# A gated mix of a spectral filter and a state-space recurrence: the issue order of all engines replaced by another one

## The chip, the cores and the metric

The kernel runs on one core of one Trainium2 chip. The metric is the device time of one execution in microseconds; a kernel's time is the median of several executions. The engines are TensorE (PE; its weight loads are PEld), VectorE (DVE), ScalarE (ACT), GpSimd (POOL) and SyncE (SP), which here only issues DMA transfers. Each engine takes its instructions strictly in the order in which they were issued, and waits at the first one whose inputs or buffers are not there.

## The reference

The input x has 2048 rows (time) and 1024 columns (features), in bf16. Two branches are computed from it and mixed by a gate of each row:

```python
g = sigmoid((x * gate_w).sum(-1, keepdims=True))
# a: spectral filter
X = rfft2(x.astype(float32), axes=(-2, -1)) * (w_r + 1j * w_i)
a = irfft2(X, s=(S, D)).astype(bfloat16)
# b: diagonal complex recurrence over the 2048 rows
h_t = Lam_bar * h_{t-1} + B_bar @ x_t
b_t = 2 * real(C @ h_t) + x_t * Dskip
out = g * a + (1 - g) * b
```

Lam_bar = exp(exp(log_dt) * Lambda) and B_bar = (Lam_bar - 1) / Lambda * B. The recurrence has 1024 complex states.

## The kernel before

The spectral branch is a chain of matrix products. x is turned on TensorE (L936, L938, tiles pt) and copied to xQ by VectorE (L947), folded (L961 to L972), transformed along the features (fd, L442 to L455, with the cast X1 on ScalarE, L461), and transformed along the rows in two steps (s1, L474, with the cast of L489; then s2, L609, after a round trip through DRAM; cast X2, L619). It is multiplied by the filter on VectorE (times_w, UV, L632), and transformed back in two steps: is1 (L648, cast C1 at L656, stored at L662 to a scratch in DRAM, read again as raw at L670) and is2 (L681, cast ZT on ScalarE, L690). Last come the groups called id (L825, L829), which ScalarE scales by the gate into BT or raw (L836) and VectorE puts together (Z and R, L844 to L865).

The recurrence branch works in 8 units of rows. The input products psu (L410, 1024 matmuls) are cast to h (L420). Each unit then goes through a list of small steps on VectorE: multiplication by tables (L340, L343), joins (L346, L349), carries (L354, L359, L380), fold_in (L362), the scan itself (L368), fill_in (L376), and the two outputs out_re (L383) and out_im (L387). One step, called next (L372), is on ScalarE between the scan and fill_in: it copies the scan's ends into the places from which fill_in reads. A step in the kernel's text is one "piece" of the list PIECES.

The products with C give y. For the tiles of 128 rows 0 to 9 they are made early: ps_y (L732, L738), scaled by the gate's other half into ye (ScalarE, L763) and stored to y_scratch in DRAM (SP, L773). The skip term is xs (loaded at L782 on SP), multiplied on VectorE (L788), scaled on ScalarE into su (L798) and added to y_scratch by an accumulating DMA issued by POOL (L804). Later POOL adds y_scratch to the finished spectral tiles (L870), and SP stores the result (L878). There are two buffers of ye and two of su: a third ye waits until a store has been read out, a third su until an accumulating DMA has. The last tiles are made at the end (ps_q, L746) and added by VectorE (L911, L918) and stored (L924).

At the start, four tables for the recurrence are made by ScalarE's sine and exponential steps (L281, L1133, L1134, L1136, L295, L296), fed by VectorE (L1129, L1131).

The order in which all of this is issued is not left to a scheduler. Three tables at the top of the file set it. ORDER is a string of some 980 characters; each stands for one kind of work (the dict `acts`), and each occurrence takes the next step of that kind, so that the letters' order is the order of issue on all five engines at once. PIECES is the order in which the letter v takes the recurrence's pieces. SLOTS says for each PSUM tile in turn which of the four PSUM slots it gets. A slot is taken by the next tile only when the last one in it has been read, so SLOTS and ORDER belong together.

```python
    for act in "".join(ORDER):
        if act == "v":
            piece(next(pieces))
        else:
            next(acts[act], None)
```

The engines wait on each other by semaphores, which are set from the data and the buffers; ORDER does not change what is computed.

Of the kernel before, what the change touches and what calls it, by code (L numbers as in the profile page):

```python
# [41 lines left out]
TURN_DVE = tuple(range(16))  # L42
CLOSES = (0, 1, 2, 3, 10, 4, 5, 11, 12, 6, 7, 8, 9)
PIECES = (
# [7 lines left out]
)  # L52
SLOTS = (
    "0123012301230123021302130231023102302302130230123013021302301201320320213023021310102312012301230210",
    "2302021302130230230213132012031203203123120310321032103210130212031203120",
)
MIRROR = (6, 7, 8, 9)
ORDER = (
    "xTxUfTUVfVVa|2xTTGfVVVrrffa|tfUUtGGFFaxEfftffTTxUESbSbtfU2fFTaxAxTffUUfrFAE2fftxSaakFtEAEtfxbbbbbtTT",
    "TFtTbEbUUbFSUUf~ttfFEufSUUU1UbSSArESttfFAAAftFtbbbttEEwttthH~tfthfftufFFSHbtAtttvfvEEtvgvbSASKhtt1r1",  # L60
    "AtAe1vttrtHtr~1vftve111~htuuhttvtFrttF1ttvtHfvthh1vv1tttEttvcEvccccvccctHvSevvSSFcHHwFAAhhEwScKvE11v",
    "KvvSccctttvvtvvAhKvHeevhvcccvv1nAA1KK1swHvvvvvHHsYvvvvkMvvvvssssvhvvvvvHvvnnLYYsvvvvvvnNWssJNsJNNvsh",
    "MhsvsvvJvsvWyHMss344jhvvMM3hHvLvv5vWmm++HnH54v56nMyvvMMWv78378v4nnmmJNvJNvv5hv5vJ56Yvhv4NJyNjYvM+vvM",
    "453WM787HH44y55hH+mm67h8Hv+n7vWm3Nn54JWYvvnvv558468+vvvhMv3vmvJj5NMMv77+8484vYnJN+ydmvyN55JWvvvHhd6h",
    "3H787mM8Hvv555+mjn6M44hYN77vv+5vm3n55HJv644dvyJ8n87N7+Jmv5v5v5vvv+8vh6NnYvym7vv878Hh8qhq+mNviqJivHh+",
    "miiiIqIniv+vHHvIIvvYyivvIJXv+IvvqvYvvnIqviXNvyiJnimqiIinmvYNIiihIIIvvvvvvvJvvNNvq%iiIIIIv++hHHlzlvpp",
    "hvllzZZPZZZZPRRQQRRRmXvHdJhRpzzDmD+ZZRZZHvPZZlJQvoRpOvQvPlDzBzZZovZvOlZpovRYRZlZDzzvvoRRBDoOOvoyQRQB",
    "BlvDDv+POBZOZRBZZvZvlZzzpvZZQDoovvQoDCZYZZooZ9PooYRyRRRDyYRRQQ9CC9000999DDD09000",
)

EVEN = ((0, 0), (2, 1), (2, 0), (0, 1))
# [1167 lines left out]
```

## Time and profile before

| | us |
|---|---|
| median of 3 executions | 301.17 |
| lowest and highest of them | 300.79, 302.21 |
| the profiled execution's own time | 303.33 |
| its span in the profile | 301.6 |
| TensorE busy | 292.6 (97%) |
| VectorE busy | 284.2 (94%) |
| ScalarE busy | 209.5 (69%) |
| GpSimd busy | 81.0 (27%) |
| granted TensorE clock | 1.000 |

The profile's page gives the busy time of every engine, groups of instructions by line, and the chain of work that ended last. A row of a timeline has the start, the duration, the engine, the line and the operation with its tiles (out<-in), and in square brackets the idle time ahead of it and what ended that. A row of the list of waits has the engine, the tile and line that waited, what it waited for, and the total, the number and the longest of such waits. A row of the table by windows has the stretch and its length, then for each engine its busy time and instructions in it, then the granted clock, the share of the DMA engines and GB/s. A DMA row's duration in the chain is from issue to landing.

### The profile page before, as it was taken

How to read it: one execution, taken by the hardware profiler on the slowest of the kernel's cores; microseconds unless marked ns; L12 is line 12 of the kernel's file. 1: busy time of each engine (PE TensorE's matmuls, PEld its weight loads, DVE VectorE, ACT ScalarE, POOL GpSimd, SP SyncE). 2: the span in 40 equal slices, each digit the busy share in tenths (PEclk: the TensorE clock that was granted, in tenths of full speed). 3: DMA queues.
4: the chain of work that ended last, by engine and by line, in shares of the span. 5: the costliest groups of instructions: out<-in, count | busy, mean ns of one | idle time of the engine just before them, and what ended most of it. 6: DMA issues, size and time to landing. Idle time of an engine off the chain costs nothing. (4 is left out here: it accounts for less than half of the span.)

```text
span 301.6 us, 6230 instructions
## 1 busy us (share of the span) xinstructions
PE 292.6 (97%) x2446; PEld 194.6 (65%) x2446; DVE 284.2 (94%) x359; ACT 209.5 (69%) x323; POOL 81.0 (27%) x107
## 2 busy tenths in 40 slices
PE   7899999999999999999999999999979999999995
PEld 4465868977764874477546754688547996556443
DVE  4999999999889999999988999999997899999994
ACT  1899999998531578757685989757969885267100
POOL 2232276696460020200310111201111042244230
PEclk9999999999999999999999999999999999999999
DMA  6999999999978779878995895878999419999995
GB/s 216 289 281 202 196 159 311 153 142 175 196 213 242 196 181 237 211 217 208 222 275 161 180 256 124 195 229 251 250 225 189 79 19 193 124 184 193 124 163 190
DMA packets 74140, 59.21 MB, mean 196 GB/s; under 512 B 44872, under 2 KB 61664, under 8 KB 74112
## 3 DMA queue, kind: packets, MB, share of 16 engines
q1 hardware_dynamic: 66560, 49.69, 64.8%
q0 software_dynamic: 6896, 8.69, 23.8%
q8 instruction: 19, 0.31, 0.5%
q10 hardware_dynamic: 656, 0.44, 0.5%
q14 instruction: 9, 0.07, 0.1%
HBM read 27.33 MB, written 23.08 MB: 167 GB/s over the span
## 5 line engine op out<-in xcount | busy, mean ns | idle before, releaser
L410 PE MATMUL psu<-xQ,BT 128*128 128x256 bf16 x1024 | 116.2, 273 | 0.0
L410 PEld LDWEIGHTS <-BT 128*128 128x128 bf16 x1024 | 98.9, 98 | 16.9 <-issue 4.2
L732 PE MATMUL ps_y<-CT,h 128*128 128x512 bf16 x416 | 93.6, 380 | 0.7 <-ACT ye L763 0.6
L732 PEld LDWEIGHTS <-h 128*128 128x128 bf16 x416 | 39.8, 98 | 47.9 <-issue 4.0
L804 POOL DMA_DIRECT2D y_scratch<-su x20 | 19.2, 987 | 122.9 <-ACT su L798 84.8
L420 ACT CAST h<-psu 128x1024 bf16<-128x1024 f32 x32 | 32.3, 1013 | 15.3 <-PE psu L410 14.6
L343 DVE TENSOR_TENSOR h<-h,tab 128x4096 bf16<-128x4096 bf16 (+1 forms) x20 | 37.4, 1870 | 0.2
L368 DVE TENSOR_TENSOR_SCAN h<-rz,h 128x512 bf16<-128x512 f32 (+1 forms) x14 | 35.9, 2584 | 0.1
L340 DVE TENSOR_TENSOR xQ<-h,tab 128x4096 bf16<-128x4096 bf16 x12 | 27.4, 2284 | 0.3 <-ACT h L420 0.2
L763 ACT ACTIVATE ye<-ps_y,omg 128x512 f32<-128x512 f32 x26 | 17.2, 682 | 12.3 <-PE ps_y L732 6.1
L372 ACT ACTIVATE xQ<-h,r_sb 128x254 bf16<-128x254 bf16 x48 | 20.5, 508 | 1.4 <-DVE h L368 1.4
L870 POOL DMA_DIRECT2D BT<-y_scratch x10 | 12.7, 1543 | 32.1 <-ACT h L420 16.7
L746 PE MATMUL ps_q<-CT,h 128*128 128x512 bf16 (+2 forms) x112 | 20.9, 349 | 0.0
L836 ACT ACTIVATE BT<-ps_id,gB 128x1024 bf16<-128x1024 f32 x14 | 14.9, 1114 | 6.0 <-DMA out_dram<-BT 6.0
L656 ACT CAST C<-ps_is 128x1024 bf16<-128x1024 f32 x16 | 15.6, 1011 | 4.6 <-PE ps_is L648 3.8
L798 ACT ACTIVATE su<-xs,omg 128x512 f32<-128x512 bf16 x20 | 14.1, 722 | 6.7 <-DVE xs L788 3.0
L619 ACT CAST X<-ps_s 128x1024 bf16<-128x1024 f32 x16 | 16.1, 1008 | 3.8 <-PE ps_s L609 2.6
L690 ACT CAST ZT<-ps_is 128x1024 bf16<-128x1024 f32 x16 | 16.8, 1125 | 0.6 <-ACT su L798 0.6
L746 PEld LDWEIGHTS <-h 128*128 128x128 bf16 x112 | 10.4, 98 | 10.5
L461 ACT CAST X<-ps_fd 128x1024 bf16<-128x1024 f32 x16 | 15.8, 1019 | 0.4 <-PE ps_fd L455 0.4
L289 POOL CAST tab<-sc 128x512 bf16<-128x512 f32 x4 | 4.9, 1234 | 23.3 <-ACT sc L1136 23.3
L947 DVE COPY xQ<-pt 128x1024 bf16<-128x1024 bf16 x12 | 7.8, 683 | 3.5 <-PE pt L938 3.5
(210 smaller groups left out, 440.8 us busy)
## 6 DMA issues: line engine op xcount, KB each, us to landing
y_scratch<-ye SPq DMA_DIRECT2D x20, 256.0 KB, 3.9
y_scratch<-su POOLq DMA_DIRECT2D x20, 256.0 KB, 6.5
Bb<-turn_scratch SPq DMA_DIRECT2D x16, 256.0 KB, 4.9
turn_scratch<-C SPq DMA_DIRECT2D x16, 256.0 KB, 3.4
raw<-turn_scratch SPq DMA_DIRECT2D x8, 512.0 KB, 5.0
xs<-in_A_x_dram SPq DMA_DIRECT2D x13, 256.0 KB, 4.4
out_dram<-BT SPq DMA_DIRECT2D x11, 256.0 KB, 4.5
CT<-in_A_x_dram SPq DMA_DIRECT2D x5, 512.0 KB, 4.7
```

Of the source, the lines that this page charges most:

```text
L340: nc.vector.tensor_mul(out=tmps["s"], in0=u[:, :, ::-1], in1=bc(i))
L343: nc.vector.tensor_mul(out=u, in0=u, in1=bc(i))
L368: nc.vector.tensor_tensor_scan(out=seg, data0=flat(rz, i), data1=seg, initial=0.0, op0=ALU.mult, op1=ALU.add)
L372: nc.scalar.activation(out=tmps["s"][:, 0, :, i, 1:TS], in_=u[:, 1, :, i, 0:TS - 1], func=ACT.Copy, scale=r2_sb[:, js.start + i:js.start + ...
L410: nc.tensor.matmul(psu[:, j, :], lhsT=BT[4 * q + j][:, ri, d8, :], rhs=xQ[:, c, d8, :], start=(d8 == 0), stop=(d8 == 7))
L420: nc.scalar.copy(out=hs[c][:, :, ri, 4 * q:4 * q + 4].rearrange("p e b (q j) -> p e b q j", j=16), in_=psus.pop((c, q, ri)).rearrange("p b ...
L619: nc.scalar.copy(out=X2s[g][:, :, b], in_=ps2s[g][b])
L690: nc.scalar.copy(out=fft["ZT"][:, kp, :, :, 2 * G:2 * G + 2], in_=pszs.pop((G, kp)).rearrange("p v (x n) -> p x n v", n=64))
L732: nc.tensor.matmul(psy, lhsT=hs[c][:, tq, ri, jb, :], rhs=CT[ri][:, jb, 512 * dh:512 * (dh + 1)], start=(i == 0), stop=(i == 15 and tb not ...
L746: nc.tensor.matmul(psq, lhsT=hs[c][:, tq, ri, jb, :], rhs=CT[ri][:, jb, at:at + n], start=(i == 0), stop=(i == 15))
L763: nc.scalar.activation(out=ye, in_=psys[tb][:, K * hf:K * (hf + 1)], func=ACT.Copy, scale=omg[:, tb:tb + 1])
L804: nc.gpsimd.dma_start(out=y_dram[tb, hf], in_=xgs[tb, hf], accum_op=ALU.add)
```

## The change

The three tables are replaced as a whole; no other line differs. The change comes with the words "Order of all engines laid anew from the last trace's durations, judged by four cases with longer transfers". The first line of each, before and after:

```diff
 PIECES = (
-    0, 1, 2, 3, 4, 5, 6, 9, 8, 10, 7, 11, 12, 13, 14, 15, 16, 18, 17, 20, 21, 22, 23, 19, 24, 25, 26, 27, 28, 29, 30,
...
+    0, 1, 2, 3, 5, 6, 8, 4, 7, 9, 10, 11, 12, 14, 13, 15, 16, 18, 17, 20, 21, 19, 24, 23, 25, 22, 26, 27, 29, 28, 30,
...
 SLOTS = (
-    "0123012301230123021302130231023102302302130230123013021302301201320320213023021310102312012301230210",
...
+    "0123012301230132013012031023103210321021302130210312013213023020132102030231231021032312032101321301",
...
 ORDER = (
-    "xTxUfTUVfVVa|2xTTGfVVVrrffa|tfUUtGGFFaxEfftffTTxUESbSbtfU2fFTaxAxTffUUfrFAE2fftxSaakFtEAEtfxbbbbbtTT",
...
+    "xxTUffTUV2VVxGf|Va|VVGTffattfUtTfataGFUfaxxr2kbFraxxxfrETTUxSESfttfAUAFET2fFtff1tTTUfFTFETUUffbbbUEt",
```

What the tables do is seen in the rows of an engine's program. A row has the line, the operation, its output and inputs, and the output's shape; the number behind a tile's name is a running one and differs between the two programs for the same tile.

On ScalarE, in the first 15 us, before: the sine step for small vectors, then the two casts X1 of fd's first tiles (L461), then three steps of the first table.

```order
L1134 ACTIVATE SC_158<-ang2_153 128x16
L461 CAST X1_285<-ps_fd_264 128x1024
L461 CAST X1_318<-ps_fd_273 128x1024
L1133 ACTIVATE rot_kk_292<-ang_255 128x512
L1134 ACTIVATE sc_291<-ang_255 128x512
L1136 ACTIVATE SC_158<-a2_kk_250,chpi_117 128x16
L489 CAST CT0_82<-ps_s1_320 128x1024
```

After, in the same place:

```order
L1134 ACTIVATE SC_158<-ang2_153 128x16
L1133 ACTIVATE rot_kk_250<-ang_243 128x512
L1134 ACTIVATE sc_249<-ang_243 128x512
L1136 ACTIVATE SC_158<-a2_kk_240,chpi_117 128x16
L461 CAST X1_317<-ps_fd_271 128x1024
L461 CAST X1_344<-ps_fd_291 128x1024
L1136 ACTIVATE sc_249<-rot_kk_250,chpi_117 128x512
L489 CAST CT0_82<-ps_s1_339 128x1024
```

The three table steps (L1133, L1134, L1136) have moved from behind the two casts to in front of them.

On SP, near 205 us of the trace before. The rows with ye are the stores of tile 7 (its two halves), those of L670 are the loads raw that is2 reads, those of L782 the loads of xs:

```order
L670 DMA raw_125<-turn2_scratch_58 128x2048 x3
L773 DMA y_scratch_60<-ye_2798 128x512
L670 DMA raw_125<-turn2_scratch_58 128x2048
L782 DMA xs_3034<-in_A_x_dram 128x1024
L773 DMA y_scratch_60<-ye_2902 128x512
L1182 DMA_TRANSPOSE xQ_121<-in_A_x_dram 128x8x128
L670 DMA raw_125<-turn2_scratch_58 128x2048
```

After:

```order
L670 DMA raw_125<-turn2_scratch_58 128x2048 x2
L773 DMA y_scratch_60<-ye_2797 128x512
L670 DMA raw_125<-turn2_scratch_58 128x2048
L782 DMA xs_3036<-in_A_x_dram 128x1024
L773 DMA y_scratch_60<-ye_2938 128x512
L670 DMA raw_125<-turn2_scratch_58 128x2048 x4
```

The store of the first half has moved one raw load forward (it stood behind three and stands behind two), the store of the second half too: before it stood behind the fourth raw load and an xs load, and now it stands behind the third and an xs load. The further raw loads follow it.

On VectorE, at the end of the last unit of the recurrence, from its fill_in (L376) on, before:

```order
L376 TENSOR_TENSOR h_3312<-h_3312,xQ_121 128x2048
L863 TENSOR_TENSOR BT_122<-BT_122 128x2x512
L340 TENSOR_TENSOR xQ_121<-h_3312,tab_123 128x4096
L865 TENSOR_TENSOR BT_122<-BT_122 128x2x512
L343 TENSOR_TENSOR h_3312<-h_3312,tab_123 128x4096
L844 TENSOR_TENSOR BT_122<-BT_122 128x2x2x128
L846 TENSOR_TENSOR BT_122<-BT_122 128x2x2x128
L387 TENSOR_TENSOR h_3312<-h_3312,xQ_121 128x2x1024
L383 TENSOR_TENSOR h_3312<-h_3312,xQ_121 128x2x1024
L911 SCALAR_TENSOR_TENSOR xQ_121<-xs_3174,omg_142,BT_122 128x1024
L855 TENSOR_TENSOR BT_122<-BT_122 128x4x256
L857 TENSOR_TENSOR BT_122<-BT_122 128x4x256
```

After:

```order
L376 TENSOR_TENSOR h_3259<-h_3259,xQ_121 128x2048
L340 TENSOR_TENSOR xQ_121<-h_3259,tab_123 128x4096
L343 TENSOR_TENSOR h_3259<-h_3259,tab_123 128x4096
L911 SCALAR_TENSOR_TENSOR xQ_121<-xs_3254,omg_142,BT_122 128x1024
L383 TENSOR_TENSOR h_3259<-h_3259,xQ_121 128x2x1024
L844 TENSOR_TENSOR BT_122<-BT_122 128x2x2x128
L387 TENSOR_TENSOR h_3259<-h_3259,xQ_121 128x2x1024
L846 TENSOR_TENSOR BT_122<-BT_122 128x2x2x128
L855 TENSOR_TENSOR BT_122<-BT_122 128x4x256
L857 TENSOR_TENSOR BT_122<-BT_122 128x4x256
L918 SCALAR_TENSOR_TENSOR raw_125<-ps_q_3743,omg_142,xQ_121 128x512
```

The sum L911 has moved from behind out_im and out_re (L387, L383) to in front of both, with the other steps of Z and R laid differently around them, and out_re goes before out_im.

More of the change, by code (lines that the diff above doesn't have):

```diff
@@ L44 @@
 PIECES = (
[7 rows of a table removed]
[7 rows of a table added]
 )
 SLOTS = (
-    "0123012301230123021302130231023102302302130230123013021302301201320320213023021310102312012301230210",
-    "2302021302130230230213132012031203203123120310321032103210130212031203120",
+    "0123012301230132013012031023103210321021302130210312013213023020132102030231231021032312032101321301",
+    "3202132032103203203120201230123023021321302130213021031203103212031202310",
 )
@@ L58 @@
 ORDER = (
-    "xTxUfTUVfVVa|2xTTGfVVVrrffa|tfUUtGGFFaxEfftffTTxUESbSbtfU2fFTaxAxTffUUfrFAE2fftxSaakFtEAEtfxbbbbbtTT",
[L60 to L68, printed above, removed]
+    "xxTUffTUV2VVxGf|Va|VVGTffattfUtTfataGFUfaxxr2kbFraxxxfrETTUxSESfttfAUAFET2fFtff1tTTUfFTFETUUffbbbUEt",
+    "SSEffAAFfUrt~fFTuUUUUffEbrbUttttbtbSbbttESASSbfAAbbbbAFEFEhttSAtffttt~uHhH~bftFEtFttutgttKSSv1th1EFe",
+    "11tv1111fv~tvA1rwAttvhhtht1cefEtvtvrcStttcStvvttvvccreHcHutttvtfvvHtvA1tHhttvFcccAvwwccFEEhhvvvSvttS",
+    "vvccFtvvvhvHvccHvAvvvvecKK1vv1vKA1KvEwSAKv1evsYYHHhHvvvvshnHvvMLvsssnvvvnnNWJvvWvsssvMhvvNvvjvsJvsvM",
+    "sshvhNyHHvsvsvkNssvWv3MvLhYMMvvnm4v4JmY5yJ++3HMHmvvn544NNJWJ5vv678v5v+vnvMm3v54vMnM56hh74+NvN8v3vyj5",
+    "78mvH+5vhh5678mvvnMvHWH445Jdd77vMYHNYWy+vJ34nm4jmN8+MJ556vnvy7+8Yvv53W4v7585nNhhJvNMvH4vm8+vJvWvv677",
+    "Hhvvv5jHmM3Mn5+454XJ86ymvN787Yhm8385vJ55H4n4Nvy6n+57hv8v5567vvvmvvvYyNnv7hvvvJ8878HhvX++mq+hqHvNmmiH",
+    "HvIJiIiIvnvvviqivivYvJynvIqvvIIviINi+vvvvqq+nmvmiqiiNniIYyIIIvJhJvNiivqivNvIYvvvHvIIiIIdv%XhvHlzlzJp",
+    "Pvl+ZZZpPm+ZZZRRzhQlzHdJvpPRhRpollQDDmHRZZ+RPZZRZvZQQDOovyvDlzzvRBvoZYZOBvpzlzoZZovDRZ+RZQQRRvOZoOlZ",
+    "vvRZZvBBRlDDooDZZQvvPvvOCBOBvzzZpQvoPZZDoZ9ZZQQY0RRRRyyRRC999CDDoo0o9099DY00D00Y",
 )
```

12 rows, old and new, of the table PIECES are left out of this document.

## Prediction

> **What bounds the kernel now.** I read the page's shares first, then the table by windows, then the timelines of the engines around each hole that the table shows, and last the chain of waits where the largest hole lies.
>
> ```profile
> span 301.6 us, 6230 instructions
> PE 292.6 (97%) x2446; PEld 194.6 (65%) x2446; DVE 284.2 (94%) x359; ACT 209.5 (69%) x323; POOL 81.0 (27%) x107
> ```
>
> TensorE is busy for 292.6 of 301.6 us, VectorE for 284.2. Both columns are nearly full, so the order can't win more than the holes that TensorE has. The table by windows shows where they are: each row is a stretch, and TensorE's hole is its length less its busy time.
>
> ```profile
> 0.00:10.00 10.00, 7.20 (x58) 4.51 (x59) 5.55 (x21) 2.95 (x9) 3.44 (x16) 1.00 0.76 240
> 10.00:20.00 10.00, 9.61 (x80) 5.51 (x79) 9.93 (x24) 9.96 (x15) 1.72 (x1) 1.00 1.11 305
> 120.00:150.00 30.00, 29.57 (x266) 18.38 (x265) 29.82 (x24) 21.14 (x33) 3.69 (x5) 1.00 0.88 209
> 150.00:200.00 50.00, 49.70 (x425) 29.56 (x425) 47.65 (x39) 39.54 (x69) 6.71 (x8) 1.00 0.79 197
> 220.00:240.00 20.00, 18.32 (x174) 14.04 (x173) 18.48 (x12) 16.71 (x25) 1.73 (x2) 1.00 0.86 177
> 280.00:302.00 22.00, 18.39 (x102) 9.09 (x99) 17.63 (x26) 0.01 (x1) 3.34 (x3) 1.00 0.80 158
> sum 302.00, PE 292.61 PEld 194.58 DVE 284.19 ACT 209.54 POOL 81.01; mean PE 24.38 PEld 16.21 DVE 23.68 ACT 17.46 POOL 6.75
> ```
>
> The table was cut so that it covers 302 us, and the holes are 302.00 − 292.61 = 9.4 us. Of these 2.80 lie in the first 10 us, where the first loads arrive, and 3.61 in the last 22, nearly all behind the last matmul, where the last tile is scaled and stored. Neither can be laid anew away. That leaves 0.39 + 0.43 + 0.30 + 1.68 = 2.8 us in between, and 1.68 of it in one place, 220 to 240 us. The granted clock (third column from the end) is 1.00 throughout. The Trainium skill, page "Perfetto Trace Analysis", section "Identifying the Most-Contended Engine", holds that busy share says little of how far TensorE is from its limit, because matmuls are pipelined, and would have us judge by the share of weight loads: 65% here, which by that rule would leave a third of the span open. The trace does not bear that out for an order alone: a change of order removes no matmul and no weight load, only holes.
>
> **The change part by part.** The code is the same; only the order is laid anew, and with it which PSUM slot a tile gets. Four places decide.
>
> The first is the start. ScalarE, VectorE and TensorE there, before:
>
> ```profile
> 11.72 1.91 ACT L461 CAST X<-ps_fd 128x1024 bf16<-128x1024 f32 x2
> 13.51 0.64 ACT L1133 ACTIVATE rot_kk<-ang 128x512 f32<-128x512 f32 x1
> 14.04 0.63 ACT L1134 ACTIVATE sc<-ang 128x512 f32<-128x512 f32 x1
> 14.56 0.30 ACT L1136 ACTIVATE SC<-a_kk,chpi 128x16 f32<-128x16 f32 x1
> ...
> 9.77 1.28 DVE L947 COPY xQ<-pt 128x1024 bf16<-128x1024 bf16 x2
> 12.09 0.69 DVE L1131 TENSOR_TENSOR ang<-ang,rot_kk 128x512 f32<-128x512 f32 x1
> ...
> 9.52 0.59 PE L455 MATMUL ps_fd<-G_sb,preT 128*128 128x512 bf16 x2 [1.03 <-DMA G_sb<-c_G]
> 13.04 1.24 PE L474 MATMUL ps_s<-X,raw 64*128 64x512 bf16 x8
> ```
>
> The two casts at 11.72 are what the first two matmul groups of s1 (L474, at 13.04) read. After, three steps of the first table stand ahead of them. By their starts in the trace they take 14.04 − 13.51 = 0.53, 14.56 − 14.04 = 0.52 and 14.76 − 14.56 = 0.20 (the next cast starts at 14.76), 1.25 us in all. Their own input, L1131 on VectorE, ends at 12.78 before; it too is moved forward, past the second copy and two fold steps, so it ends at some 11.4 and makes no wait of its own. The first cast then starts at 12.97. Before, it ended near 12.7 (half of the 1.91) and s1 began at 13.04, behind other work of TensorE, so 0.3 of the 1.25 is slack for the first group; the second group reads the second cast, which ended at 13.63, and began near 13.66, half-way through its row's 1.24, so there is none. TensorE loses about 1.25, and 0.95 if the first group alone counts. The G loads' waits (1.03 and another) keep their place on the queue and stay. Behind this, TensorE has no hole larger than 0.3 up to 149 us, so what it loses stays lost, less about 0.15 of small holes (the 0.39 of the 10-to-20 row) that a later TensorE no longer finds. I take **+1.1** (ends +0.7 and +1.25).
>
> The second is at 149. Before, on TensorE and ScalarE:
>
> ```profile
> 148.95 0.62 PE L609 MATMUL ps_s<-Bb,KRS_sb 64*32 64x512 bf16 x16
> 150.13 2.10 PE L732 MATMUL ps_y<-CT,h 128*128 128x512 bf16 x9 [0.56 <-ACT ye L763]
> ...
> 148.78 0.72 ACT L798 ACTIVATE su<-xs,omg 128x512 f32<-128x512 bf16 x1 [1.25 <-DVE h L368]
> 149.41 0.67 ACT L763 ACTIVATE ye<-ps_y,omg 128x512 f32<-128x512 f32 x1
> ```
>
> TensorE waits 0.56 for ye, and ye stood behind su, which took 149.41 − 148.78 = 0.63 of ScalarE. After, this su stands elsewhere, and ye stands directly behind a cast that is long done. It can go as soon as the y group ends, at 148.95, which is 0.46 earlier. **−0.4** (ends 0 and −0.56).
>
> The third is the large hole. The chain of waits, then ScalarE, then TensorE:
>
> ```profile
> 205.42 0.32 SPq L670
> 205.78 1.45 SPq L782
> 207.27 6.59 DMA y_scratch<-ye
> 214.40 8.28 DMA y_scratch<-su
> 222.77 0.72 ACT su L798
> ...
> 202.23 0.67 ACT L763 ACTIVATE ye<-ps_y,omg 128x512 f32<-128x512 f32 x1
> 219.26 1.09 ACT L690 CAST ZT<-ps_is 128x1024 bf16<-128x1024 f32 x1
> ...
> 222.21 0.61 PE L681 MATMUL ps_is<-KRS_sb,raw 128*128 128x128 bf16 x8
> 224.11 0.61 PE L681 MATMUL ps_is<-KRS_sb,raw 128*128 128x128 bf16 x8 [1.30 <-ACT ye L763]
> 225.10 0.61 PE L681 MATMUL ps_is<-KRS_sb,raw 128*128 128x128 bf16 x8 [0.38 <-ACT ZT L690]
> 225.54 3.62 PE L732 MATMUL ps_y<-CT,h 128*128 128x512 bf16 x16
> ```
>
> It begins on SP. The ye tile was ready at 202.90, yet its store went out at 207.27, because a raw load (205.42) and an xs load (205.78) stood in front and the first of them waited for its buffer. The store took 6.59, the accumulating DMA on the same rows 8.28, and su at 222.77, which needs the buffer that this DMA reads, waited from 220.35 (219.26 + 1.09) on. With it waited ye, the ZT casts and TensorE. A group of eight takes 225.54 − 225.10 = 0.44 without a wait, so TensorE loses 224.11 − 222.21 − 0.44 = 1.46 and 225.10 − 224.11 − 0.44 = 0.55, together 2.0. After, that raw load stands behind the store and only the raw load before it and the xs load in front. I put the store at 204.5 to 205.0, so at least 2.3 earlier: landed near 211.5, accumulated by 222.77 − 2.4 = 220.4 if both transfers take as long as before. That meets the 220.35 at which su wants the buffer, and su itself, being behind a TensorE that is 0.7 late, asks later. The wait goes: **−2.0** (ends −2.0 and −0.3, if the transfers take longer). Next late there is a ZT cast that now stands behind six steps of the recurrence instead of two, by 0.2 at most in a count of the work ahead: **+0.2**.
>
> The fourth is the end. VectorE and TensorE before:
>
> ```profile
> 281.69 1.22 DVE L383 TENSOR_TENSOR h<-h,xQ 128x2048 bf16<-128x2048 bf16 x1
> 284.02 0.69 DVE L855 TENSOR_TENSOR BT<-BT 128x1024 bf16<-128x1024 bf16 x1
> ...
> L746 PE MATMUL ps_q<-CT,h x112: 218/379/380, 277.5 to 298.2; 128*128 128x512 bf16 x80, 128*128 128x384 bf16 x16, 128*128 128x128 bf16 x16
> ```
>
> L746 has 7 blocks of 16 matmuls, in columns as much as 80 + 12 + 4 = 96 matmuls of 512; from 277.5 to 298.2 that is 20.7 / 96 = 0.216 each, so the two blocks of tile 13 fill 32 × 0.216 = 6.9 us, 277.5 to 284.4, and there the blocks of tile 14 begin, which read what L387 and L383 leave, the last at 281.69 + 1.22 = 282.9. The slack is 1.5. After, L911 (1.20, from 282.82, where L383 gives way, to 284.02) stands in front of both, some steps that stood in front stand behind, and over all of VectorE's rows 0.8 more of work stands ahead of the last of them, by a sum of the same rows' durations; 0.7 stays. One of TensorE's last id groups moves from before tile 13's blocks to behind them, so that what VectorE makes of it comes later, yet still ahead of its last use: **0** (ends 0 and +1, if VectorE is late by what it waits below).
>
> The rest are many moves of one or two steps in the middle, where TensorE has no hole now. They add work nowhere. Two places get tighter. An su step now follows directly on the one before it, though it must wait for the accumulating DMA that reads its buffer, and the recurrence has less other work of VectorE between a scan and the fill_in behind it. I take **0** for TensorE, with ends of −0.3 (the hole of the 150-to-200 row goes) and +1.0.
>
> The sum against the profiled run is +1.1 − 0.4 − 2.0 + 0.2 = −1.1, and I keep 0.1 for small new holes, so −1.0. The profiled execution took 303.33 us, 1.7 of it outside its span of 301.6; the span becomes 300.6 and that run's time 302.3. The median of the three timed runs is 301.17, 2.2 below the profiled one, and the holes are the same work in both, so the forecast is 301.17 − 1.0 = **300.2 us**, 0.3% less. A difference of 0.5%, 1.5 us, is about what a measurement of this kernel can tell from no change (its three runs spread over 300.79 to 302.21).
>
> **The rivals.** *The start costs nothing.* If the first groups wait anyway for something that comes as late as the casts, or TensorE finds other work there, the +1.1 goes; with the 149 and 222 holes and the small ones won in full (−0.4, −2.0, −0.3) the time is 301.17 − 2.7 = 298.5. For it speaks that SP has one transpose load less in front of the first x loads, so what follows at 14 to 20 us may come earlier. Against it speaks that s1's operand is the cast itself, and no row shows TensorE waiting for a load at that point.
>
> *The store is earlier, the landing is not.* In the large hole the two transfers took 6.59 and 8.28, against medians over the whole program of
>
> ```profile
> y_scratch<-ye SPq DMA_DIRECT2D x20, 256.0 KB, 3.9
> y_scratch<-su POOLq DMA_DIRECT2D x20, 256.0 KB, 6.5
> 200.00:220.00 20.00, 20.00 (x184) 14.74 (x182) 19.64 (x18) 16.85 (x24) 1.73 (x2) 1.00 0.99 252
> ```
>
> since the engines were taken for 0.99 of that stretch. If the earlier store meets the loads that now follow it (four raw loads stand in a row), it may land as late as before: nothing of the 2.0 is won, and +1.1 − 0.4 + 0.2 makes 301.17 + 0.9 = 302.1. [...] The trace speaks for half of it (0.99), but the 4.4 us between 202.90 and 207.27 were waiting on SP and not transfer, and those go.
>
> *VectorE becomes the bound.* This is the one on the other side. VectorE is at 94%, and it stands still for the recurrence in two places only,
>
> ```profile
> DVE h L376 <- ACT su L372: 1.8, 1, 1.8
> DVE h L376 <- ACT xQ L372: 1.5, 1, 1.5
> ```
>
> where fill_in (L376) waits for ScalarE's step behind a scan. After, the cover between a scan and its fill_in is thinner in the units of the first chunks, and ScalarE itself may stand still behind the accumulating DMA that an su now waits for. If this adds two waits of 1.5 to 1.8 to VectorE and 0.8 comes from L911, VectorE is 3.8 to 4.4 later, relative to TensorE, at its last outputs; beyond the slack of 1.5 each microsecond stands at the end in full. With a middling 4.1 that is +2.6, and −1.0 becomes +1.6; with a part of the 2.0 lost as well (0.4), 301.17 + 2.0 = 303.2. It decides from 0.7 us of new VectorE waits on. For it speaks the 94%; against it, that each recurrence has a lead over its readers in the middle and that VectorE waits for the id groups (L844 for L836) after the large hole, so that what it loses ahead of that is partly lost anyway.
>
> That the change does nothing can't be: every engine's order differs from the first microseconds on.
>
> **How the numbers follow.** I give my forecast (300.2, its own range 299.3 to 301.4 by the ends of its terms) 0.42, the free start (298.5) 0.25, the late landing (302.1) 0.13, VectorE as the bound (303.2) 0.20. Faster by over 0.5% means under 299.7: nearly all of the free start, 0.22, and 0.11 of the forecast, 0.33 together. Slower by over 0.5% means above 302.7: 0.17 of VectorE's case, 0.03 of the late landing and 0.02 of the forecast, 0.22. The rest is 0.45. The range goes from 297.6, below the free start by the small holes of the middle, to 303.4, above VectorE's case by a little; longer waits of VectorE are left outside, with about 0.1 to either side.
>
> **What would show it.** In the table by windows of the changed kernel, the row of 0 to 20 us should show TensorE about 1.1 less busy, with s1 (L474) starting at 14.0 and waiting for the cast of L461; the 220-to-240 row should have TensorE at 19.8 or more, the wait of su (L798) for y_scratch's DMA be gone from the list of waits, and the ye store of the chain be issued before 205.5. Around 149 the wait for ye should be under 0.2. L746 should run without a hole from 277 on. The forecast is wrong if L474 starts at 13.1 (free start), if su still waits for the DMA around 220 (late landing), or if L746 has a hole that ends with a VectorE L383 or L387, and L376's waits are longer (VectorE).

## The result, and the profile after

The changed kernel takes 304.26 us (median of 7, 303.48 to 304.99), the kernel before 301.17 (median of 7, 300.65 to 303.04). The ratio is 1.0088, with a 95% interval of 1.0059 to 1.0118: slower by 0.9%, outside the range of the prediction. (The quotient of the two medians is 1.0103, inside that interval.) On the chips of the later comparisons the kernel before took 300.8.

The profiled execution of the changed kernel took 303.59 us, 0.2% less than its median. The first lines of its page, then its table by windows. The page has 2425 matmul records where that of before has 2446; a hole of 0.1 us in this trace can be a missing record.

```profile
span 301.8 us, 6205 instructions
PE 291.6 (97%) x2425; PEld 194.8 (65%) x2446; DVE 284.8 (94%) x359; ACT 208.8 (69%) x323; POOL 74.2 (25%) x107
```

```profile
10.00:20.00 10.00, 8.56 (x78) 5.71 (x79) 9.90 (x31) 9.91 (x17) 1.89 (x3) 1.00 1.17 271
120.00:150.00 30.00, 29.90 (x273) 18.51 (x281) 29.89 (x26) 23.25 (x40) 2.57 (x3) 1.00 0.95 221
200.00:220.00 20.00, 18.76 (x169) 14.00 (x170) 18.07 (x15) 13.77 (x21) 2.47 (x3) 1.00 0.86 235
220.00:240.00 20.00, 19.62 (x189) 14.91 (x188) 19.06 (x13) 19.80 (x30) 1.75 (x2) 1.00 0.76 192
```

Read against the rows of before, the holes are where the prediction said, and where it did not. Of TensorE's busy time the start lost 1.05 (9.61 to 8.56; 1.1 was forecast), 120 to 150 gained 0.33, and 220 to 240 gained 1.30 (to 19.62; 19.8 was forecast). But 200 to 220, which had no hole, now has one of 1.24. By spans the two profiled executions are alike, 301.6 and 301.8; by medians they are 3 us apart. The step from the one to the other is the first thing that the experiments had to settle.

What opened between 200 and 220, on ScalarE, then POOL, SP and TensorE:

```profile
198.86 0.72 ACT L798 ACTIVATE su<-xs,omg 128x512 f32<-128x512 bf16 x1
202.94 0.72 ACT L798 ACTIVATE su<-xs,omg 128x512 f32<-128x512 bf16 x1
208.44 0.72 ACT L798 ACTIVATE su<-xs,omg 128x512 f32<-128x512 bf16 x1 [4.79 <-DMA y_scratch<-su]
209.07 1.91 ACT L420 CAST h<-psu 128x1024 bf16<-128x1024 f32 x2
...
199.88 0.86 POOL L804 DMA_DIRECT2D y_scratch<-su  x1 [7.02 <-ACT su L798]
...
203.07 0.32 SPq L773 DMA_DIRECT2D y_scratch<-ye  x1
...
210.11 0.61 PE L681 MATMUL ps_is<-KRS_sb,raw 128*128 128x128 bf16 x8 [0.82 <-ACT h L420]
211.03 3.61 PE L732 MATMUL ps_y<-CT,h 128*128 128x512 bf16 x15 [0.31 <-ACT h L420]
```

The su of tile 6's second half is made at 198.86; its accumulating DMA goes out at 199.88 and lands 8.5 us later, at 208.4. The su of tile 7's second half needs that buffer and stands 4 us behind, so ScalarE stops for 4.79 us, with two h casts and the ZT casts behind it, and TensorE stops for them. The store that the prediction wanted early is early (203.07, against 207.27), so the hole at 222 is not there. The same kind of wait has come up one tile ahead.

### The profile page after: what moved, and what is told of

The parts are those of the page before. It is cut to its first block, busy times and chain, and to the rows that moved or that the text cites. A ratio compares the mean times of both kernels' runs of the same rounds, so it can differ in the third digit from the quotient of the medians.

```text
span 301.8 us, 6205 instructions
## 1 busy us (share of the span) xinstructions
PE 291.6 (97%) x2425; PEld 194.8 (65%) x2446; DVE 284.8 (94%) x359; ACT 208.8 (69%) x323; POOL 74.2 (25%) x107
## 4 chain that ended last, share of the span: by engine, by line
PE 72%; ACT 13%; DVE 5%; DMA 5%; POOL 2%; issue 2%; ACTq 0%
PE ps_y L732 29%; PE psu L410 22%; PE ps_q L746 7%; DMA z_scratch<-zsb 3%; PE ps_id L829 2%; DVE h L368 2%; ACT h L420 2%; ACT X L461 2%; DMA y_scratch<-ye 2%; PE ps_fd L455 2%; POOL tab L300 1%; PE ps_is L648 1%; PE ps_s L609 1%; PE ps_id L825 1%; PE ps_is L681 1%
## 5 line engine op out<-in xcount | busy, mean ns | idle before, releaser
L410 PE MATMUL psu<-xQ,BT 128*128 128x256 bf16 x1024 | 115.4, 273 | 0.3 <-ACT ZT L690 0.3
L410 PEld LDWEIGHTS <-BT 128*128 128x128 bf16 x1024 | 99.2, 98 | 16.1 <-issue 3.8
L732 PE MATMUL ps_y<-CT,h 128*128 128x512 bf16 x400 | 92.5, 379 | 1.4 <-ACT h L420 0.3
L461 ACT CAST X<-ps_fd 128x1024 bf16<-128x1024 f32 x16 | 15.8, 1017 | 1.6 <-PE ps_fd L451 1.3
L300 POOL TENSOR_SCALAR tab<-sc,rinv 128x256 bf16<-128x256 f32 x8 | 10.6, 1330 | 4.6 <-ACT sc L295 4.5
```

Source lines behind the costliest of these rows:

```text
L410: nc.tensor.matmul(psu[:, j, :], lhsT=BT[4 * q + j][:, ri, d8, :], rhs=xQ[:, c, d8, :], start=(d8 == 0), stop=(d8 == 7))
L461: (nc.vector.tensor_copy if j in FD_DVE else nc.scalar.copy)(out=X1.rearrange("p r (m e c) -> p r m e c", e=2, c=2), in_=psf.pop(j).rearra ...
L732: nc.tensor.matmul(psy, lhsT=hs[c][:, tq, ri, jb, :], rhs=CT[ri][:, jb, 512 * dh:512 * (dh + 1)], start=(i == 0), stop=(i == 15 and tb not ...
```

## The experiments

Every ratio is to the kernel before on the same chip, with its 95% interval. The edits move steps in ORDER alone. Diffs show the issue order of one engine, as far as it moved.

**The kernel before, unchanged.** 

> The kernel before, unchanged. First theory (the large hole of the profiled execution is not in most executions): this trace, if its time is near 301, has no TensorE hole above 0.5 us between 220 and 226 us. Rival (the hole is in every execution, and the changed kernel loses elsewhere): a hole of about 2.0 us there whatever the time. The ratio to the kernel before is 1.000 within its interval either way.

Measured: 300.74 us, ratio 0.9995 (0.9985 to 1.0004). Of its profiled execution, which took 300.76: the span, TensorE's window at the large hole, and the su and the DMA there.

```profile
span 299.0 us, 6207 instructions
220.00:240.00 20.00, 19.95 (x195) 16.04 (x195) 19.62 (x14) 18.76 (x26) 1.73 (x2) 1.00 0.76 153
213.03 0.86 POOL L804 DMA_DIRECT2D y_scratch<-su  x1 [5.97 <-DMA y_scratch<-ye]
219.75 0.72 ACT L798 ACTIVATE su<-xs,omg 128x512 f32<-128x512 bf16 x1
```

The accumulating DMA goes out at 213.03, 1.4 us earlier than in the profile of the prediction, and lands after 5.8 us instead of 8.3; su at 219.75 follows without a wait. TensorE's hole in that window is 0.05 instead of 1.68. The large hole belonged to the execution of 303.33 us and is not in the usual one: the 11 executions of this run took 300.62 to 300.94. On the chip of the first comparison 302.21, 302.99 and 303.04 are on record for the kernel before too, 3 of 7; whether these had the hole was not traced.

**The start put back, on ScalarE (changed kernel).**

```diff
 L1134 ACTIVATE SC<-ang_153 128x16
+L461 CAST X_304<-ps_fd 128x1024
+L461 CAST X_331<-ps_fd 128x1024
 L1133 ACTIVATE rot_kk<-ang 128x512
 L1134 ACTIVATE sc<-ang 128x512
 L1136 ACTIVATE SC<-a_kk,chpi 128x16
-L461 CAST X_317<-ps_fd 128x1024
-L461 CAST X_344<-ps_fd 128x1024
```

> The changed kernel with one thing undone: ScalarE's three table steps (L1133, L1134, L1136) and the small vector steps stand behind the first two casts L461 again. If the start's 1.25 us stays lost to the end, the time falls from 304.26 by 1.0 to 1.25, to 303.1. If later waits swallow it (something else sets the end), it falls by less than 0.5.

Measured: 304.22 us, ratio 1.0117 (1.0103 to 1.0130); nothing won. The changed kernel was not run again on this chip or the later ones, so what a run wins over its 304.26 compares two chips. TensorE in this run:

```profile
16.20 0.61 PE L938 MATMUL pt<-ident_g,CT 128*128 128x128 bf16 x8 [0.74 <-ACT CT L489]
19.28 0.61 PE L445 MATMUL ps_fd<-G_sb,preT 128*128 128x256 bf16 x4 [0.28 <-DVE preT L968]
```

It reaches s1 earlier and meets two waits that the late start had covered.

**The su behind the casts (changed kernel).**

```diff
 L763 ACTIVATE ye<-ps_y,omg 128x512
-L798 ACTIVATE su<-xs,omg 128x512 x2
+L798 ACTIVATE su<-xs,omg 128x512
 L420 CAST h<-psu 128x2x512 x2
 L690 CAST ZT<-ps_is_2941 128x512x2
 L690 CAST ZT<-ps_is_2961 128x512x2
+L798 ACTIVATE su<-xs,omg 128x512
```

> The changed kernel with one step of ScalarE moved: the su (L798) that waits 4.79 us for the accumulating DMA at 203.6 to 208.4 stands behind two h casts and two ZT casts instead of in front of them. First theory: the TensorE holes at 208 to 211 (1.46 us) go and the time falls from 304.26 to about 302.8. Rival (the wait moves to the next place that needs the buffer): a hole of over 1 us appears at 211 to 226 and the time falls by less than 0.5.

Measured: 302.97 us, ratio 1.0075 (1.0062 to 1.0087): 1.3 us less than the changed kernel by medians. The interval of this ratio lies within that of the changed kernel (1.0059 to 1.0118), so the times alone do not settle it; the run after this one makes the same move on this chip. TensorE runs through at 208 us, and su needs no wait:

```profile
211.61 0.74 ACT L798 ACTIVATE su<-xs,omg 128x512 f32<-128x512 bf16 x1
208.55 1.50 PE L681 MATMUL ps_is<-KRS_sb,raw 128*128 128x128 bf16 x24
```

TensorE's hole between 200 and 220 us falls from 1.24 to 0.44; 0.33 of what is left is a new wait for a ZT cast, at 219.5.

**Both edits.** 

> Both of these edits together. First theory: they add up, 304.26 - 1.1 - 1.5 = 301.7, within 0.3% of the kernel before. Rival (something else, spread over the middle, makes the changed kernel slow): 303 or more.

Measured: 303.30 us, ratio 1.0091 (1.0076 to 1.0107). Not 301.7: the start gives nothing here either. Against the run with the start put back alone (304.22, on this chip) the su wins 0.9.

**The next steps behind two casts (with the su moved).**

```diff
+L420 CAST h<-psu 128x2x512 x2
 L372 ACTIVATE su<-h,r2_sb 128x2x127 x4
-L420 CAST h<-psu 128x2x512 x2
```

> The changed kernel with the su step moved as in the run before (302.97), and also two h casts (L420) of unit 1 moved ahead of the next steps (L372) that wait 3.4 us for the scan at 66 to 70 us. Theory (the in-order wait holds back the casts, and TensorE loses about 0.7 us at 72 to 79): 302.97 falls by about 0.5, to 302.4. Rival (VectorE's own lateness sets that stretch): no change, 302.9.

Measured: 302.43 us, ratio 1.0055 (1.0042 to 1.0067), another 0.54 less, by medians on two chips. ScalarE around the wait in the changed kernel, then in this run:

```profile
69.77 1.70 ACT L372 ACTIVATE su<-h,r_sb 128x254 bf16<-128x254 bf16 x4 [3.43 <-DVE h L368]
71.37 1.90 ACT L420 CAST h<-psu 128x1024 bf16<-128x1024 f32 x2
```

```profile
66.18 1.03 ACT L420 CAST h<-psu 128x1024 bf16<-128x1024 f32 x1
68.73 1.01 ACT L420 CAST h<-psu 128x1024 bf16<-128x1024 f32 x1 [1.52 <-PE psu L410]
70.02 1.70 ACT L372 ACTIVATE su<-h,r_sb 128x254 bf16<-128x254 bf16 x4 [0.28 <-DVE h L368]
```

The first cast now runs at 66.18, where the wait for next had kept it until 71.37. TensorE needs the casts' PSUM slots: in the run before, it waited 0.30 us at 73.63 for the second cast, and in this one it does not.

**The changed start, in the kernel before.**

```diff
-L461 CAST X_285<-ps_fd 128x1024
-L461 CAST X_318<-ps_fd 128x1024
 L1133 ACTIVATE rot_kk<-ang 128x512
 L1134 ACTIVATE sc<-ang 128x512
 L1136 ACTIVATE SC<-a_kk,chpi 128x16
+L461 CAST X<-ps_fd 128x1024 x2
```

> The kernel before with the changed kernel's start alone: the three table steps ahead of ScalarE's first two casts, and VectorE's small vector steps early. The prediction's term: +1.1 us, 302.0. What the two traces suggest instead (TensorE's holes behind it shrink by as much): +0.3 at most, 300.9 to 301.2.

Measured: 302.06 us, ratio 1.0045 (1.0033 to 1.0057). Here it costs what the prediction said, 1.3 us. TensorE's wait, and then where the first unit product (L410) starts in this run, in the unchanged kernel before and in the changed kernel (behind the durations stand its first and its last start):

```profile
14.03 0.61 PE L474 MATMUL ps_s<-X,raw 64*128 64x512 bf16 x4 [1.23 <-ACT X L461]
L410 PE MATMUL psu<-xQ,BT x1024: 269/273/283, 31.8 to 247.4; 128*128 128x256 bf16 x171
```

```profile
L410 PE MATMUL psu<-xQ,BT x1024: 269/273/283, 30.6 to 246.1; 128*128 128x256 bf16 x171
```

```profile
L410 PE MATMUL psu<-xQ,BT x1024: 269/273/283, 31.0 to 249.6; 128*128 128x256 bf16 x171
```

Alone the start delays the first unit product by 1.2 us; in the changed kernel, whose steps behind it are laid for it, by 0.4. But the first unit product stands in another place of TensorE's order there, with less work ahead of it. By TensorE's holes in the first 30 us, five traces with the old start lie at 3.1 to 3.9 us (mean 3.5), the four of the changed kernel with its start as it is at 3.7 to 4.5 (mean 4.2): the start costs it about 0.7, not 0.4. The two traces of the old order with the changed start lie at 4.2 and 4.5, so by this measure it costs about as much in either order.

**The store ahead of the raw load, in the kernel before.**

```diff
 L670 DMA raw<-turn_scratch 128x2048 x3
-L773 DMA y_scratch<-ye 128x512
+L773 DMA y_scratch<-ye 128x512 x2
 L670 DMA raw<-turn_scratch 128x2048
 L782 DMA xs<-in_A_x_dram 128x1024
-L773 DMA y_scratch<-ye 128x512
```

> The kernel before with one store (L773, second half of tile 7) moved ahead of the fourth raw load on SP, the mechanism of the prediction's largest term. The prediction's term: -2.0 us, 298.9. Theory now (the hole is not in the usual execution, so there is nothing to win): within 0.3 us of the kernel before.

Measured: 300.83 us, ratio 1.0000 (0.9990 to 1.0011). The store goes out 5 us earlier than in the unchanged kernel's usual execution (206.58). The accumulating DMA behind it, the second of the row of POOL, goes out at 207.1 instead of 213.03 and lands after 8.0 us instead of 5.8, so 3.7 us earlier. Nobody waits for it: su is made at the same time, 219.71 against 219.75.

```profile
201.61 0.32 SPq L773 DMA_DIRECT2D y_scratch<-ye  x1
206.25 1.75 POOL L804 DMA_DIRECT2D y_scratch<-su  x2 [13.36 <-DMA y_scratch<-ye]
219.71 0.72 ACT L798 ACTIVATE su<-xs,omg 128x512 f32<-128x512 bf16 x1
```

**One su later, in the kernel before.**

```diff
-L798 ACTIVATE su<-xs,omg 128x512
 L656 CAST C<-ps_is 128x1024
 L656 CAST C<-ps_is 128x1024
 L420 CAST h<-psu 128x2x512
-L798 ACTIVATE su<-xs,omg 128x512
+L798 ACTIVATE su<-xs,omg 128x512 x2
```

> The kernel before with one su step (L798, second half of tile 6) moved behind the C1 casts and the first h cast, so that its accumulating DMA starts some 7 us later and the next su of the same buffer comes about 4 us behind it on ScalarE, as in the changed kernel. Theory (this distance is what the changed kernel lost): a wait of 2 to 5 us for the DMA in front of L798 at 203 us, a TensorE hole near 208, and 0.7 to 2 us more than before. Rival (the wait is hidden, the hole comes from elsewhere): within 0.3 us of the kernel before.

Measured: 302.63 us, ratio 1.0063 (1.0051 to 1.0075), 1.9 us by medians. The wait of the changed kernel is there, behind a DMA that goes out at 198.93 and lands after 7.9 us:

```profile
206.93 0.72 ACT L798 ACTIVATE su<-xs,omg 128x512 f32<-128x512 bf16 x1 [4.47 <-DMA y_scratch<-su]
208.67 0.61 PE L681 MATMUL ps_is<-KRS_sb,raw 128*128 128x128 bf16 x8 [0.33 <-ACT ZT L690]
211.45 1.89 PE L732 MATMUL ps_y<-CT,h 128*128 128x512 bf16 x7 [0.31 <-ACT h L420]
```

**The first su earlier (changed kernel).** The su of 198.86 goes ahead of the two C1 casts and the h cast. It then also stands ahead of an accumulating DMA that should have read its buffer first, so one half tile gets a wrong skip term; the amount of work is the same.

> The changed kernel with one su step (L798, second half of tile 6) moved the other way, ahead of two C1 casts and two h casts, as in the kernel before; the su that waited stays where it is. Theory (what counts is the distance on ScalarE between two su of one buffer against the DMA's landing): the accumulating DMA goes out at 193 instead of 200, lands before 203.6, the wait of 4.8 us in front of L798 and the holes at 208 to 211 go, and the time is 302.9 to 303.1, as with the later su. Rival (the transfer takes its 8 us wherever it is put, or the su has to wait elsewhere): 304 or more.

Measured: 302.69 us, ratio 1.0060 (1.0048 to 1.0072). The two su of tile 7 now run back to back:

```profile
203.65 1.33 ACT L798 ACTIVATE su<-xs,omg 128x512 f32<-128x512 bf16 x2
208.94 1.50 PE L681 MATMUL ps_is<-KRS_sb,raw 128*128 128x128 bf16 x24
```

So it is the distance that counts: moving either su apart from the other takes the wait away, and by medians wins 1.3 to 1.6 us.

**The start put back in full, ScalarE.** The fourth step of the table (L1136) moves behind the A1 and X1 casts as well; this run has the later su and the two h casts ahead of next too. 

> The changed kernel with the two edits of the run that took 302.43, and the start undone in full: ScalarE's first two casts ahead of the three table steps, as before, and the table's fourth step (L1136 for the whole table) behind the next A1 and X1 casts as well, which in the first try at the start stood in front of an A1 cast for which TensorE waited 0.74 us. Theory (that wait took the gain of the first try): 302.43 falls by 0.7 to 1.2, to 301.2 to 301.7. Rival (the start is bound by something else there): 302.2 or more.

Measured: 302.73 us, ratio 1.0066 (1.0054 to 1.0078). The rival holds. TensorE waits at once for VectorE:

```profile
19.79 0.61 PE L445 MATMUL ps_fd<-G_sb,preT 128*128 128x256 bf16 x4 [0.95 <-DVE preT L968]
```

**A ye behind the h cast (with the three edits before).**

```diff
-L763 ACTIVATE ye<-ps_y,omg 128x512
...
+L690 CAST ZT<-ps_is_3218 128x512x2
 L420 CAST h<-psu 128x2x512
-L690 CAST ZT<-ps_is_3218 128x512x2
+L763 ACTIVATE ye<-ps_y,omg 128x512
```

> The same, and at 228 to 234 us one ye (L763) behind the h cast and one ZT cast ahead of it, since TensorE waited 0.38 us there for ZT. If ScalarE's order is the cause, 0.3 to 0.5 less than the run of three edits; if ScalarE has simply no time left in that stretch, no change.

Measured: 306.77 us, ratio 1.0202 (1.0189 to 1.0215), 4 us worse than with the three edits: a miss of mine. The is2 group behind needs the PSUM slot that this ye empties, which SLOTS had laid down. TensorE, and its window right behind the hole:

```profile
234.85 2.71 PE L681 MATMUL ps_is<-KRS_sb,raw 128*128 128x128 bf16 x24 [2.67 <-ACT ye L763]
235.00:238.00 3.00, 3.00 (x28) 2.80 (x27) 3.00 (x3) 2.11 (x3) 0.00 (x0) 0.50 0.87 234
```

The hole makes 2.3 of the 4 us. From 235 to 238 us the granted clock is 0.50, and the 24 matmuls take 2.71 us instead of the 1.50 of the other runs; over the whole execution TensorE is busy 1.6 us longer for the same 2446 matmuls. All four executions have a mean granted clock of 0.993 or 0.994.

**Both pieces in the kernel before.** 

> The kernel before with two pieces of the change put in: the start (alone +1.3) and the later su (alone +1.9). Theory (both are holes of TensorE, far apart, with no slack between them that takes one up): they add, 300.8 + 3.2 = 304.0, about the changed kernel's time. Rival (a later TensorE no longer meets the second wait): 302.7 or less.

Measured: 303.96 us, ratio 1.0098 (1.0081 to 1.0115): the two add, and the sum is about the changed kernel's time. Single executions lay at 301.87 to 304.23, and the profiled one was that of 301.87, with a short wait and no hole:

```profile
206.05 0.72 ACT L798 ACTIVATE su<-xs,omg 128x512 f32<-128x512 bf16 x1 [1.73 <-DMA y_scratch<-su]
209.33 1.50 PE L681 MATMUL ps_is<-KRS_sb,raw 128*128 128x128 bf16 x24
```

The accumulating DMA landed after 5.9 us here, against 7.9 with the later su alone. So the wait's price hangs on how long one transfer takes in that execution.

**The start put back on both engines, three ways.** VectorE's small steps move behind the folds too. 

> The run that took 302.43 (later su, two h casts ahead of next) with the start undone on both engines: ScalarE's first two casts ahead of the table steps, and VectorE's ten small vector steps (1.3 us) behind the fold steps that TensorE waits for, as in the kernel before. Theory (the start costs 1.2 on ScalarE, and undoing it there alone only shows the same lateness on VectorE): 302.43 falls to 301.2 to 301.5. Rival (the start of the changed kernel is bound by neither, and its cost is not to be had back): 302.2 or more.

> The same, with the su of tile 6 early and its predecessor's accumulating DMA ahead of it (so that the skip term is right), and the su that waited at its place in the changed kernel. If distance alone counts, the same time as the run beside it within 0.3 us: 301.2 to 301.5. If the later su was worth more than the wait, more than that.

> The run that took 302.43 once more with the start undone on both engines, and the first table's scaling (L295, L296), which in the last try waited 2.7 us on ScalarE for VectorE's small steps with casts behind it, moved behind the casts that TensorE waits for. If those waits took the gain (0.9 us at 16 us in that trace), the time is 301.3 to 301.8. If the changed kernel's order behind the start is bound to its later start (rival), another wait within 20 us takes it, and the time is 302.2 or more.

Measured: 305.58 (1.0124, 1.0087 to 1.0160), 305.01 (1.0107, 1.0074 to 1.0140) and 304.38 us (1.0117, 1.0100 to 1.0133), all worse than the 302.43 that they started from. Of the six executions of each of the first two, four had a mean granted clock of 0.994 and took 304.90 to 306.06; the two at 1.000 took 304.51 and 304.55, and 303.96 and 303.99. In the first, ScalarE waits for the small steps; in the third, that wait is gone and TensorE waits for a cast behind the table's scaling instead:

```profile
ACT t L296 <- DVE ci L1166: 2.7, 1, 2.7
```

```profile
28.45 1.47 PE L474 MATMUL ps_s<-X,raw 64*128 64x512 bf16 x12 [1.43 <-ACT X L461]
```

The second carries the first's wait, so its time says little on the two su; it lies 0.6 from the first. Its trace shows the two su of tile 7 without a wait, here with the right skip term:

```profile
204.76 1.33 ACT L798 ACTIVATE su<-xs,omg 128x512 f32<-128x512 bf16 x2
```

**The second term alone, in the kernel before.**

```diff
-L798 ACTIVATE su<-xs,omg 128x512
 L763 ACTIVATE ye<-ps_y,omg 128x512
+L798 ACTIVATE su<-xs,omg 128x512
```

> The kernel before with the second term of the prediction alone: the su (L798) at 148.8 us behind the ye (L763) for which TensorE waits 0.56 us there. The prediction's term: -0.4, 300.4. Rival (the hole comes back at the next wait): within 0.1 of the kernel before.

Measured: 300.88 us, ratio 0.9996 (0.9972 to 1.0020). TensorE's wait for ye in the unchanged kernel's usual execution, and in this run:

```profile
149.88 3.40 PE L732 MATMUL ps_y<-CT,h 128*128 128x512 bf16 x15 [0.22 <-ACT ye L763]
```

```profile
149.66 3.61 PE L732 MATMUL ps_y<-CT,h 128*128 128x512 bf16 x16 [0.22 <-ACT ye L763]
```

The 0.56 of the prediction was 0.22 already, and stays 0.22. The interval is too wide to tell 0.4 us from nothing; the rows show that the hole was not there to be won.

No version here beats the kernel before; the best of the changed kernel's, 302.43, is 1.7 behind it.

## Why the prediction was wrong

**The step that failed first is "the holes are the same work in both".** The profiled execution took 303.33 us, and the three timed runs lay at 300.79 to 302.21. I carried its holes over to the median unchanged. Its surplus of 2.2 was nearly the very holes that I meant to close: the usual execution has neither the 2.0 at 222 nor most of the 0.56 at 149.

**Third term, −2.0.** The mechanism in that profile was read rightly, and the store did move the way it was said to. Making the same move in the kernel before wins 0.0 (0.9990 to 1.0011): in the usual execution nobody waited for that transfer. The rival that the store would be earlier and its landing not is wrong there, since the accumulating DMA landed 3.7 us earlier. In place of the gain stands a loss that I priced at nothing: I followed tile 8's su back to its DMA, and not tile 7's, though the order puts tile 6's second su behind the C1 casts and tile 7's two su close behind that. The sentence on an su directly behind the one before it, waiting for the DMA, stands among the "many moves", with an end of +1.0 and a value of 0. By medians it is worth 1.3 us by moving the later su, 1.6 by moving the earlier one (both against the changed kernel's time on another chip; 0.9 on one chip, with the start put back), and 1.9 when put into the kernel before.

**First term, +1.1.** Right in size for the move by itself (1.3 us in the kernel before), and right in its place: s1 starts at 14.0 as forecast. Somewhat too large in the sum, since the steps behind it were laid anew too: by TensorE's holes up to 30 us it is about 0.7. The runs that put the start back did not get it back: each met other waits in the first 32 us. So whether this order can do without the loss stays open.

**Second term, −0.4.** The usual execution has 0.22 of this hole, and moving su leaves it as it is. The time of that run (0.9972 to 1.0020) could not have told 0.4 us from nothing.

**Fourth term, 0.** Right. The last blocks in the changed kernel:

```profile
L746 PE MATMUL ps_q<-CT,h x110: 219/379/379, 277.1 to 298.4; 128*128 128x512 bf16 x78, 128*128 128x384 bf16 x16, 128*128 128x128 bf16 x16
```

From first to last start that is 21.3 us, 0.6 more than before, and one id group now stands within it. VectorE did not become the bound: its waits in front of fill_in (L376) are 3.7 us in all, against 3.3 before. So the rival on the slower side had the sign by the wrong mechanism.

**The middle, 0.** Wrong by 0.5: next waits 3.4 us for its scan with two casts behind it, worth 0.54 by medians on two chips (the hole that goes with it is 0.30). The end of +1.0 that I gave it was not in the sum. The +0.2 for a late ZT cast was about right in size, as TensorE's row there shows; the run that moved a ye to mend it opened a larger hole.

```profile
234.63 3.65 PE L410 MATMUL psu<-xQ,BT 128*128 128x256 bf16 x32 [0.33 <-ACT ZT L690]
```

**The range.** The upper ends that I gave the terms add up to 301.17 + 1.25 + 0 − 0.3 + 0.2 + 0.1 + 1 + 1 = 304.4, so the 301.4 of my forecast's own range is not their sum. The measured 304.26 lies inside the sum and outside the range.

**What remains.** By the runs, 1.3 for the su and 0.5 for next make 1.8 of the 3.5 us between 304.26 and 300.8. The remaining 1.7 is what 302.43 still has over the kernel before. By windows it lies in two places. The unchanged kernel before (the execution of 300.76), then the run of 302.43:

```profile
0.00:30.00 30.00, 26.64 (x221) 16.48 (x225) 25.30 (x72) 22.35 (x35) 8.52 (x25) 1.00 0.98 246
200.00:240.00 40.00, 39.84 (x373) 30.56 (x375) 38.46 (x31) 36.09 (x50) 3.45 (x4) 1.00 0.88 212
```

```profile
0.00:30.00 30.00, 25.60 (x218) 16.07 (x222) 25.38 (x71) 22.59 (x37) 8.22 (x23) 1.00 1.05 257
200.00:240.00 40.00, 39.14 (x366) 29.73 (x368) 37.82 (x27) 34.84 (x50) 3.99 (x5) 1.00 0.80 213
```

Up to 30 us TensorE's holes differ by 1.04 (some 0.3 of that is how these two executions happened to start, by the means above), and from 200 to 240 by 0.70, which is two waits for ZT casts, 0.33 and 0.38. Between 30 and 200 us the run of 302.43 has 0.2 less of holes. The pages of the two have 2423 and 2425 matmul records, so missing records do not make the difference. This says where the time is; no run won it back.

## What to carry to other kernels

A hole in a profile counts in full only if that execution's time is that of the usual one: where it lies above the timed runs, take the surplus off the holes first, or look at a second execution. When an order is laid anew, go through every wait of a buffer that a DMA must free, not only the ones that waited before: in-order engines pay not for the wait but for what stands behind it. What a piece costs alone in the old order need not be what the new order gives back without it: the start cost 1.3 us there, and putting it back here won nothing. And where two orders differ, compare the holes up to a time, not the start of one instruction.

## What the runs showed of the hardware

The same accumulating DMA of 256 KB took 8.3 us from issue to landing in one execution of the kernel before (issue at 214.40) and 5.8 in another (issue at 213.03). Another one, with a buffer that is wanted again within that spread, landed after 7.9 us with the later su alone (an execution of 302.63 us) and after 5.9 with the start as well (one of 301.87). Six executions of that last program lay at 301.87 to 304.23; its slower ones were not traced. The kernel before itself lay at 300.56 to 302.06 over 26 executions on one chip, and at 300.46 to 303.64 over 17 on another; what made its slow ones slow was traced only for that of 303.33.

The granted clock fell to 0.50 for 3 us right behind a wait of TensorE of 2.67 us (the run with the ye moved), and to a mean of 0.66 between 25 and 30 us behind waits of 0.64 and 1.66 us (the first of the three ways to put the start back). The second of the three ways had the same two waits, and its traced execution kept 1.00. Read so, a hole of this length can cost more than its length, though not in every execution; these are two traces, and no run was made to test it.
